# The last tile's 32-row stores on ScalarE's queue beside SyncE's

## The chip, the cores and the metric

The kernel runs on one core of a Trainium2 chip. The metric is the device time of one execution in microseconds (us).

## The reference

A block-sorted attention is followed by an affine mixer. What matters here is its last line, which gives the kernel's output of 4 batches × 768 tokens × 512 channels:

```python
def _moe_ref(x, alpha1, beta1, w_tok, alpha2, beta2, w_ch1, w_ch2, lam):
    ...
    ch = np.maximum(a2 @ w_ch1, 0.0) @ w_ch2
    return (u + lam * ch).astype(np.float32)
```

## The kernel before

The 768 tokens of a batch stand in six tiles of 128 rows. A tile holds 96 rows from the first 576 tokens and 32 rows from the last 192 (the "tail"), so a finished tile goes to the output in two stores, one of 96 rows and one of 32. The very last tile of the program is also cut by columns, into 384 and 128, so that the first part can be finished and stored while TensorE still multiplies the second. All output stores are issued by SyncE.

```python
    def moe_ch(b, hf, kks=range(3)):
        ...
            last = b == B - 1 and kt == NT - 1
            ost = att.tile([128, C], FT, name="ost", tag="ost", bufs=2)
            for lo, hi in ((0, 384), (384, C)) if last else ((0, C),):
                cps = psb([128, hi - lo], FT, "ch_ps")
                for m in range(HT):
                    pe.matmul(cps[:], hT[m][...], W2p[:, m, lo:hi], ...)   # cut
                dve.tensor_tensor(cps[:], cps[:], lamB[:, lo:hi], ALU.mult)
                dve.tensor_tensor(ost[:, lo:hi], cps[:], u_of[b][kt][:, lo:hi], ALU.add)
                nc.sync.dma_start(out[b, kt * 96:(kt + 1) * 96, lo:hi], ost[0:96, lo:hi])
                nc.sync.dma_start(out[b, TAIL + kt * 32:TAIL + (kt + 1) * 32, lo:hi], ost[96:128, lo:hi])
```

The softmax here doesn't subtract the row's maximum and nothing guards it: scores larger than these inputs give would overflow.

Of the kernel before, what the change touches and what calls it, by code (L numbers as in the profile page):

```python
# [16 lines left out]
def kernel(  # L17
# [20 lines left out]
    nc = tc.nc  # L38
# [13 lines left out]
    TAIL = 6 * BLK  # L52
# [35 lines left out]
    def psb(shape, dtype, name):  # L88
        return psB.tile(shape, dtype, name=name, tag="psB")

    def const(shape, dtype, name):
# [5 lines left out]
        out=ident16[:], in_=ident16[:], compare_op=ALU.not_equal, fill=1.0, base=0,  # L97
# [554 lines left out]
    def moe_ch(b, hf, kks=range(3)):  # L652
        hT = hT_of[(b, hf)]
        for kk in kks:
            kt = 3 * hf + kk
# [5 lines that stand above are left out]
                    pe.matmul(  # L661
                        cps[:], hT[m][:, kk * 128:(kk + 1) * 128], W2p[:, m, lo:hi],
                        start=(m == 0), stop=(m == HT - 1),
                    )
                dve.tensor_tensor(cps[:], cps[:], lamB[:, lo:hi], ALU.mult)
                dve.tensor_tensor(ost[:, lo:hi], cps[:], u_of[b][kt][:, lo:hi], ALU.add)
                nc.sync.dma_start(out[b, kt * 96:(kt + 1) * 96, lo:hi], ost[0:96, lo:hi])
                nc.sync.dma_start(out[b, TAIL + kt * 32:TAIL + (kt + 1) * 32, lo:hi], ost[96:128, lo:hi])


    ets = {}
# [86 lines left out]
    for kk in range(2):  # L758
        moe_ch(0, 0, (kk,))
        mix_k(1, gs=((0, 1), (2,))[kk])  # L760
        for h4 in range(2 * kk, 2 * kk + 2):
            turn_q(1, h4, dve.tensor_copy)
    pe.fixed = False
    for b in range(1, B):
        if b > 1:
            if b > 2:
                cross_q(b)
            mixing_matrices(b)
            mix_v(b)
            if b == 2:  # L770
                opened = pool.tensor_copy(gate[:], Vs[0][0:1, 0, 0:2])
                with tc.issue_after(opened.ins):
                    load_q(3)
                    load_raw(3, 1)
                    load_raw(3, 0)
            mix_k(b)
        emit_attention(b)
        if b == 1:
            moe_ch(0, 0, (2,))
        else:  # L780
            moe_h(b - 1, 0)
            moe_ch(b - 1, 0)
        moe_h(b - 1, 1)
        moe_a(b)
        moe_ch(b - 1, 1)
        if b == 1:
            load_q(2)
            cross_q(2)
# [33 lines left out]
```

## Time and profile before

| | before |
|---|---|
| median of 3 runs | 269.02 us (268.73 to 269.4) |
| span of the profiled execution | 266.8 us, granted clock 1.000 |
| TensorE (PE) busy | 257.3 us, 96% of the span |
| last matmul's end to the program's end | 4.30 us |

From the page of the kernel before, the line of PE's busy time (us, share of the span, instructions) and the line of the chain that ended last (share of the span by engine):

```profile
PE 257.3 (96%) x2049; PEld 141.6 (53%) x2059; DVE 154.8 (58%) x333; ACT 125.8 (47%) x232; POOL 92.6 (35%) x100
...
PE 89%; ACT 4%; DVE 4%; issue 1%; DMA 1%; DVEq 0%; ACTq 0%
```

TensorE bounds the kernel; no change to the last stores touches that. What they can change is the stretch after the last matmul. The timeline of that stretch in the kernel before follows (start in us from the span's start, duration in us, engine, line, operation, what it writes and reads; SPq is SyncE issuing a store, and ACTq, further on, ScalarE issuing one):

```profile
262.10 0.39 PE L65 MATMUL ch_ps<-W2p,hTb 128*128 128x128 bf16 x4
262.30 0.56 DVE L65 TENSOR_TENSOR ost<-ch_ps,u 128x384 f32<-128x384 f32 x1
...
262.89 0.32 SPq L667 DMA_DIRECT2D out_dram<-ost  x1
263.10 0.29 DVE L65 TENSOR_TENSOR ost<-ch_ps,u 128x128 f32<-128x128 f32 x1
263.26 0.42 SPq L668 DMA_DIRECT2D out_dram<-ost  x1
263.77 0.38 SPq L667 DMA_DIRECT2D out_dram<-ost  x1
264.20 0.43 SPq L668 DMA_DIRECT2D out_dram<-ost  x1
```

VectorE finishes the 384 columns at 262.86 and the 128 columns at 263.39 (263.10 + 0.29). The four stores leave one after the other. The last one is issued at 264.20, 0.8 us after its data were ready. More readings belong to it: the view of DMA issues (KB each, median us from issue to landing), SyncE's own waits (us in total, times, the longest), and the view by windows (the last two columns are the busy share of the 16 DMA engines and GB/s).

```profile
out_dram<-ost SPq DMA_DIRECT2D x1, 144.0 KB, 1.9
out_dram<-ost SPq DMA_DIRECT2D x2, 48.0 KB, 1.7
out_dram<-ost SPq DMA_DIRECT2D x1, 16.0 KB, 1.5
```

```profile
SPq L817 <- DMA out_dram<-ost: 0.6, 2, 0.3
```

```profile
264.25:264.50 0.25, 0.00 (x0) 0.00 (x0) 0.00 (x0) 0.00 (x0) 0.00 (x0) 1.00 0.62 203
264.50:264.75 0.25, 0.00 (x0) 0.00 (x0) 0.00 (x0) 0.00 (x0) 0.00 (x0) 1.00 0.27 74
264.75:265.00 0.25, 0.00 (x0) 0.00 (x0) 0.00 (x0) 0.00 (x0) 0.00 (x0) 1.00 0.52 135
265.00:265.25 0.25, 0.00 (x0) 0.00 (x0) 0.00 (x0) 0.00 (x0) 0.00 (x0) 1.00 0.21 49
```

(The two stores of 48 KB are one line here; 1.7 is the median of 1.74 and 1.61.) The last store, 16 KB, lands 1.5 us after its issue, at 265.7. SyncE hardly waits for landings (0.6 us): its last issue ends 1.24 us after VectorE's last result, until 1.49 us it checks other semaphores, and the first store has landed at 1.39 us. The DMA engines have a dip at 264.50 to 264.75: the first two stores are nearly done, and the third store's packets begin only at 264.64.

In this trace each of these stores raises its own semaphore by sixteen increments; its landing is the time of the sixteenth.

### The profile page before, as it was taken

The numbers are of one execution on the slowest core, as the hardware profiler recorded it, in microseconds if no ns is written. First come the engines' busy times: TensorE is split into PE (matmuls) and PEld (weight loads), VectorE is DVE, ScalarE is ACT, GpSimd is POOL, SyncE is SP. The second block draws the span as 40 slices with busy tenths as digits, with TensorE's granted clock in tenths as the row PEclk, the third lists the DMA queues.
The fourth block names the chain that finished last, engine by engine and source line by source line (L and its number), as shares of the span: only waits on it lengthen the run. The fifth ranks groups of instructions, "written<-read, shape, count | busy, mean of one in ns | idle before, by whom it ended". The sixth has DMA issues, their size and how long they took to land.

```text
span 266.8 us, 5147 instructions
## 1 busy us (share of the span) xinstructions
PE 257.3 (96%) x2049; PEld 141.6 (53%) x2059; DVE 154.8 (58%) x333; ACT 125.8 (47%) x232; POOL 92.6 (35%) x100
## 2 busy tenths in 40 slices
PE   7799999999999999999999999999999999999993
PEld 3467745565565444554565444554565445545542
DVE  6878687639567966722585867704675962042033
ACT  3376767642585312980375404970474305505600
POOL 8524789103585615008918125002409000000000
PEclk9999999999999999999999999999999999999999
DMA  6999999989999544499996342492200422012012
GB/s 80 183 208 252 206 211 207 209 209 118 206 165 146 115 83 120 115 83 95 207 196 135 61 100 80 118 109 51 81 1 2 86 71 79 2 39 79 2 39 79
DMA packets 62423, 30.88 MB, mean 116 GB/s; under 512 B 48888, under 2 KB 58112, under 8 KB 62400
## 3 DMA queue, kind: packets, MB, share of 16 engines
q0 software_dynamic: 23024, 15.60, 39.1%
q1 hardware_dynamic: 39376, 14.96, 32.7%
q8 instruction: 16, 0.26, 0.4%
q14 instruction: 7, 0.06, 0.1%
HBM read 32.78 MB, written 8.65 MB: 155 GB/s over the span
## 4 chain that ended last, share of the span: by engine, by line
PE 89%; ACT 4%; DVE 4%; issue 1%; DMA 1%; DVEq 0%; ACTq 0%
PE ch_ps L65 31%; PE h_ps L65 30%; PE tok_ps L65 12%; PE x_ps L65 5%; PE sc_ps L65 4%; ACT kT L65 2%; PE v_ps L65 2%; PE k_ps L65 1%; PE q_ps L65 1%; ACT et L65 1%; DVE csum L65 1%; DVE P L65 1%; PE m_ps L65 1%; DVE rsum L65 1%; PE wtok_ps L65 1%
## 5 line engine op out<-in xcount | busy, mean ns | idle before, releaser
L65 PE MATMUL h_ps<-a2T,W1p 128*128 128x384 bf16 x512 | 93.4, 326 | 0.2
L65 ACT ACTIVATE hTa<-h_ps 128x384 bf16<-128x384 f32 x96 | 45.9, 492 | 67.7 <-PE h_ps L65 66.6
L65 PE MATMUL ch_ps<-W2p,hTa 128*128 128x512 bf16 (+2 forms) x290 | 65.9, 370 | 0.5
L65 PEld LDWEIGHTS <-W1p 128*128 128x128 bf16 x512 | 47.5, 98 | 30.3 <-issue 0.9
L65 DVE TENSOR_TENSOR ch_ps<-ch_ps,lamB 128x512 f32<-128x512 f32 (+2 forms) x25 | 16.9, 676 | 62.8 <-PE ch_ps L65 60.1
L65 POOL TENSOR_SCALAR u<-b1lB,rs 128x512 f32<-128x512 f32 x18 | 28.9, 1612 | 64.7 <-DVE ost L65 60.1
L65 PEld LDWEIGHTS <-hTa 128*128 128x128 bf16 x300 | 28.7, 98 | 32.4
L65 PE MATMUL tok_ps<-x,w_tokT 128*128 128x512 f16 x144 | 32.1, 379 | 0.0
L65 POOL TENSOR_TENSOR u<-x,u 128x512 f32<-128x512 f16 x22 | 25.4, 1190 | 18.2 <-DVE x L65 17.3
L65 ACT ACTIVATE et<-sc_ps 96x768 f16<-96x768 f32 x32 | 24.9, 807 | 11.7 <-PE sc_ps L65 11.7
L65 ACT CAST u<-u 128x512 f16<-128x512 f32 x24 | 14.8, 618 | 25.7 <-DVE u L65 25.7
L65 PE MATMUL ch_ps<-W2p,hTb 128*128 128x512 bf16 (+2 forms) x100 | 25.0, 371 | 0.0
L65 PEld LDWEIGHTS <-w_tokT 128*128 128x128 f16 x180 | 14.8, 97 | 16.1
L65 DVE TENSOR_TENSOR tok_ps<-tok_ps,a1lB 128x512 f32<-128x512 f32 x24 | 16.6, 693 | 7.7 <-PE tok_ps L65 7.6
L65 DVE CAST kT<-k_ps 64x512 f16<-64x512 f32 x24 | 16.5, 688 | 3.4 <-PE k_ps L65 3.0
L65 DVE TENSOR_TENSOR x<-x_ps,recip 96x512 f16<-96x512 f32 (+2 forms) x32 | 17.6, 554 | 0.9
L65 DVE TENSOR_TENSOR u<-tok_ps,u 128x512 f32<-128x512 f32 x24 | 16.4, 689 | 1.7
L65 ACT ACTIVATE hTb<-h_ps 128x384 bf16<-128x384 f32 x32 | 15.3, 497 | 3.8 <-PE h_ps L65 3.4
L65 DVE TENSOR_TENSOR ost<-ch_ps,u 128x512 f32<-128x512 f32 (+2 forms) x25 | 16.6, 665 | 0.6
L65 POOL DMA_DIRECT2D qn<-in_q_dram x18 | 15.4, 872 | 4.2 <-PE q_ps L65 3.4
L65 PEld LDWEIGHTS <-hTb 128*128 128x128 bf16 x100 | 9.6, 98 | 10.9
L65 PEld LDWEIGHTS <-et 96*128 96x128 f16 (+2 forms) x288 | 12.4, 99 | 4.6 <-issue 1.2
(95 smaller groups left out, 214.0 us busy)
## 6 DMA issues: line engine op xcount, KB each, us to landing
out_dram<-ost SPq DMA_DIRECT2D x23, 192.0 KB, 2.2
raw<-in_v_dram POOLq DMA_DIRECT2D x8, 384.0 KB, 8.2
raw<-in_k_dram POOLq DMA_DIRECT2D x8, 384.0 KB, 10.7
vscr<-vA SPq DMA_DIRECT2D x6, 384.0 KB, 4.4
Vs<-vscr SPq DMA_DIRECT2D x6, 384.0 KB, 7.5
W1p<-in_moe_w_ch_dram POOLq DMA_DIRECT2D x4, 512.0 KB, 10.5
W2p<-in_moe_w_ch_dram POOLq DMA_DIRECT2D x4, 512.0 KB, 18.6
qn<-in_q_dram POOLq DMA_DIRECT2D x12, 128.0 KB, 5.8
```

Of the source, the lines that this page charges most:

```text
L65: ins = getattr(self.eng, name)(*args, **kwargs)
```

## The change

With two engines issuing, the 32-row store need not wait for the issue of the 96-row store, nor the second pair for the first. ScalarE has nothing else to do by then.

```diff
                 nc.sync.dma_start(out[b, kt * 96:(kt + 1) * 96, lo:hi], ost[0:96, lo:hi])
-                nc.sync.dma_start(out[b, TAIL + kt * 32:TAIL + (kt + 1) * 32, lo:hi], ost[96:128, lo:hi])
+                (nc.scalar if last else nc.sync).dma_start(
+                    out[b, TAIL + kt * 32:TAIL + (kt + 1) * 32, lo:hi], ost[96:128, lo:hi]
+                )
```

## The prediction

> **What bounds the kernel now.** TensorE. The page gives PE 257.3 us busy of a span of 266.8 us (96%), at a granted clock of 1.00 in the view of cores, and the chain that ended last is 89% PE. The change touches only the end. The timeline of the last microseconds reads: the last matmul group starts at 262.10 and takes 0.39 us; VectorE multiplies and adds the 384 columns (0.57 + 0.56 us, done 262.86), then the 128 columns (0.29 + 0.29 us, done about 263.39). SyncE issues four stores one after the other: 262.89 (96 rows, 384 columns, 0.32 us), 263.26 (32 rows, 0.42 us), 263.77 (96 rows, 128 columns, 0.38 us), 264.20 (32 rows, 0.43 us). The third store's data are ready at about 263.39, but SyncE is still busy with the second until 263.68. So serial issue holds the third store back by about 0.35 us, and the fourth by about 0.8 us. The DMA view gives 1.9, 1.7, 1.6 and 1.5 us from issue to landing; the fourth store therefore lands last, at about 265.7. Drains and barrier semaphores then run from 266.0 to 266.8.
>
> **What the change does.** It moves two of the four issues to ScalarE's queue (its last activation starts at 252.13). All bytes and all compute stay.
>
> **Cost.** The Trainium skill, "DMA: Bandwidth & Descriptors", section "Issuing engines are not separate DMA queues", says that all issuers share the same 16 DMA engines and that issuing from several saves only the sequencer's time. This trace agrees: issues of 0.32 to 0.43 us delay the last store, while the view by windows has the engines idle from 262.5 to 263.5. With two issuers I expect: 262.89 on both queues, then about 263.42 on both, each 0.3 to 0.45 us. The last issue starts 264.20 - 263.42 = 0.78 us earlier. Not all comes back: the stores now overlap more on the 16 engines (which already moved 250 to 290 GB/s from 263.75 to 264.25), so I take landing of the last stores to lengthen by 0.1 to 0.3 us. Gain on the span: about 0.5 us, estimated from these durations; all of it is on the critical path, as nothing else runs then. That is 0.2% of 269.02 us, about the spread of the three runs (268.73 to 269.4).
>
> What could eat it: the skill's "Perfetto Trace Analysis", section "DMA Instruction — HWDGE (DVE, Sync)", says the descriptor generator is locked for exclusive use by one issuer. The trace of before has no two such issuers to show it. If the lock covers most of an issue, the four issues still follow each other, the last starts at about 264.0, and the gain shrinks to 0.1 to 0.2 us.
>
> **Prediction.** 268.5 us, 8 in 10 between 267.9 and 269.2. Faster by over 2%: 1%. Within 2%: 97%. Slower by over 2%: 2%.
>
> **What would show it.** Right: two stores on ScalarE's queue starting within 0.1 us of SyncE's; the last issue near 263.4 instead of 264.2; last landing near 265.2; span near 266.3; PE busy unchanged. Lock story: issues on the two queues lengthened to 0.6 to 0.8 us, or staggered. Contention story: early issues but landings well over 1.9 us.
>
> **What would make it wrong.** An extra queue that costs setup or extra waits at the program's end; a scheduler that orders other instructions differently because two issues changed engine; a slow first issue on ScalarE of a microsecond or more. Within 2% stands unless these cost over 5 us.

## More of the kernel before

For finer comparisons I read the trace's records directly: the instructions' starts, the packets' times, and the semaphore increments.

## The result, and the profile after

| | before | after |
|---|---|---|
| median of 6 runs | 269.15 us (268.73 to 269.4) | 268.78 us (268.55 to 268.91) |
| ratio | | 0.9986, 95% interval 0.9973 to 0.9999 |
| span of the profiled execution | 266.8 us | 266.8 us |

A ratio is the mean time of one kernel's fast runs over the mean of the other's fast runs of the same rounds, so it is not quite the ratio of the medians. The verdict is "the same" (within 2%), at 0.37 us less by the medians. Five more rounds later (run again, below) gave a ratio of 1.0002, 0.9962 to 1.0042: a gain of this size cannot be resolved by timing, so what follows rests on the end of the traces.

In the two traces the work of TensorE, VectorE and GpSimd stands in the same order; on ScalarE two stores are added after its last activation, and the same two are missing on SyncE. In the first profile after, VectorE's last result came at 263.56, 0.17 us later than before, although nothing up to there had changed. Over the profiles that moment lies between 263.39 and 264.34 (in drop_two alone, profiled in an execution of 271.96 us at a mean clock of 0.986, at 267.1). That is more than the change moves, so the spans say nothing, and I count from VectorE's last result instead.

The timeline after, first the merged lines of the first and second store of each engine (x2), then from 263.45 on, so that the second stores stand alone:

```profile
262.47 0.56 DVE L65 TENSOR_TENSOR ost<-ch_ps,u 128x384 f32<-128x384 f32 x1
...
263.06 0.85 SPq L667 DMA_DIRECT2D out_dram<-ost  x2
263.06 0.91 ACTq L668 DMA_DIRECT2D out_dram<-ost  x2
```

```profile
263.27 0.29 DVE L65 TENSOR_TENSOR ost<-ch_ps,u 128x128 f32<-128x128 f32 x1
263.59 0.32 SPq L667 DMA_DIRECT2D out_dram<-ost  x1
263.59 0.38 ACTq L668 DMA_DIRECT2D out_dram<-ost  x1
```

Both engines issue at 263.06, and both issue again at 263.59, 0.03 us after VectorE's last result. The issues are as early as they can be. The last one comes 0.77 us sooner than before, counted from VectorE's last result. The same three views as before:

```profile
out_dram<-ost SPq DMA_DIRECT2D x1, 144.0 KB, 2.1
out_dram<-ost ACTq DMA_DIRECT2D x1, 48.0 KB, 2.2
out_dram<-ost SPq DMA_DIRECT2D x1, 48.0 KB, 1.9
out_dram<-ost ACTq DMA_DIRECT2D x1, 16.0 KB, 2.1
```

```profile
SPq L819 <- DMA out_dram<-ost: 1.5, 2, 1.2
```

```profile
264.25:264.50 0.25, 0.00 (x0) 0.00 (x0) 0.00 (x0) 0.00 (x0) 0.00 (x0) 1.00 0.98 289
264.50:264.75 0.25, 0.00 (x0) 0.00 (x0) 0.00 (x0) 0.00 (x0) 0.00 (x0) 1.00 0.91 281
264.75:265.00 0.25, 0.00 (x0) 0.00 (x0) 0.00 (x0) 0.00 (x0) 0.00 (x0) 1.00 0.48 129
265.00:265.25 0.25, 0.00 (x0) 0.00 (x0) 0.00 (x0) 0.00 (x0) 0.00 (x0) 1.00 0.02 6
```

The reader should see three things. The landings of all stores are longer (2.1, 2.2, 1.9 and 2.1 us instead of 1.9, 1.7, 1.6 and 1.5). SyncE's wait for landings grew from 0.6 to 1.5 us: the issue time that was saved became waiting. And the dip of the DMA engines at 264.50 to 264.75 is filled (share 0.91 instead of 0.27; 0.65 where the window is moved by the 0.17 us by which VectorE's last result is later): the stores now overlap on the engines.

The account in us after VectorE's last result, from the trace's records:

| | before | after | after, run again |
|---|---|---|---|
| last issue (16 KB) | 0.802 | 0.032 | 0.031 |
| its time to landing | 1.493 | 2.068 | 1.993 |
| last landing | 2.295 | 2.100 | 2.024 |
| last landing to the program's end | 1.103 | 1.157 | 1.152 |
| program's end | 3.398 | 3.257 | 3.176 |

Of 0.77 us, the longer landing takes back 0.58 or 0.50. Another 0.05 us goes after the landing: SyncE checks the semaphores one by one, about 0.06 us each, in an order fixed by the program. Before, three checks are left when the last landing is seen; after, four, because the store that lands last is checked one place earlier. What is left is 0.14 us in one profile and 0.22 us in the other (0.21 us in run primed, whose last tile is the same). The kernel before was profiled once.

### The profile page after: what moved, and what is told of

Same layout as the page of the kernel before. It is cut to its first block, busy times and chain, and to the rows that moved or that the text cites. A ratio compares the mean times of both kernels' runs of the same rounds, so it can differ in the third digit from the quotient of the medians.

```text
span 266.8 us, 5149 instructions
## 1 busy us (share of the span) xinstructions
PE 257.6 (97%) x2049; PEld 141.6 (53%) x2059; DVE 154.8 (58%) x333; ACT 125.8 (47%) x232; POOL 92.5 (35%) x100
## 4 chain that ended last, share of the span: by engine, by line
PE 89%; ACT 4%; DVE 4%; issue 1%; DMA 1%; DVEq 0%; ACTq 0%
PE ch_ps L65 31%; PE h_ps L65 30%; PE tok_ps L65 12%; PE x_ps L65 5%; PE sc_ps L65 4%; ACT kT L65 2%; PE v_ps L65 2%; PE k_ps L65 1%; PE q_ps L65 1%; ACT et L65 1%; DVE csum L65 1%; DVE P L65 1%; PE m_ps L65 1%; DVE rsum L65 1%; DMA P<-in_sort_net_dram 1%
```

## The experiments

The question is why the landing grew. Three theories: shared transfer (the stores' bytes queue behind one another on the 16 engines), a slow queue (ScalarE's queue, or its first store, is slower in itself), and the descriptor generator (the prediction's fear: only one engine at a time can have a transfer set up). Diffs are against the changed kernel. "End" is the time from VectorE's last result to the program's end, from one profile each. The kernel before was timed in the same rounds; all outputs were correct except where said. The runs come from three chips, which matters little for the tail: primed and again, with the same last tile on two of them, agree to 0.01 us.

| run | last issue | last landing | end | ratio to before (95%) |
|---|---|---|---|---|
| before | 0.80 | 2.30 | 3.40 | |
| after | 0.03 | 2.10 | 3.26 | 0.9986 (0.9973 to 0.9999) |
| again | 0.03 | 2.02 | 3.18 | 1.0002 (0.9962 to 1.0042) |
| drop_one | 0.40 | 1.89 | 3.11 | 0.9987 (0.9952 to 1.0022) |
| drop_two | 0.03 | 1.79 | 3.06 | 1.0004 (0.9958 to 1.0049) |
| swap | 0.03 | 1.91 | 3.07 | 0.9985 (0.9951 to 1.0020) |
| pieces_one | 2.64 | 4.12 | 5.46 | 1.0075 (1.0063 to 1.0087) |
| pieces_two | 0.87 | 2.53 | 3.66 | 1.0016 (1.0003 to 1.0028) |
| last_only | 0.37 | 2.00 | 3.10 | 0.9992 (0.9979 to 1.0005) |
| primed | 0.03 | 2.03 | 3.18 | 0.9994 (0.9980 to 1.0008) |
| act_only | 0.89 | 2.40 | 3.50 | 1.0002 (0.9973 to 1.0030) |

The three runs with cut VectorE work follow at the end; they are counted from the last matmul.

### again: the changed kernel once more

No edit.

> The changed kernel once more, for the size of its gain and for how far one profile differs from another. In the first profiles the last landing came 2.30 us after VectorE's last result before the change and 2.10 us after it, although the last issue came 0.77 us sooner. Expected if the profiles are typical: the same 2.1 us within 0.15 us, a last store that needs 2.0 to 2.1 us from issue to landing, and a time 0.1 to 0.4 us under the kernel before. If the first profile was an outlier, the landing takes 1.6 to 1.8 us.

The profile repeated: 2.02 us to the last landing, the 16 KB store at 1.99 us. The time did not show a gain (median 268.96 us against 268.86 us). The first profile was typical to 0.08 us. The two timings agree within their intervals, and together they show no gain that is clear of noise.

### pieces_one and pieces_two: is issuing parallel at all?

```diff
+                for n in range(4 if last else 0):
+                    row = kt * 96 + n * 32 if n < 3 else TAIL + kt * 32
+                    nc.sync.dma_start(                                  # pieces_one
+                    (nc.scalar if n % 2 else nc.sync).dma_start(        # pieces_two
+                        out[b, row:row + 32, lo:hi], ost[n * 32:(n + 1) * 32, lo:hi]
+                    )
                 # cut: the last tile skips the usual two stores
```

> The cost of issuing made large: the last tile's stores are cut into pieces of 32 rows, four for each part of the columns, eight in all, all on SyncE. Same bytes. All theories: eight issues of about 0.42 us one after another, the last about 2.6 us after VectorE's last result; last landing about 4.1 us after it; slower than the kernel before by about 1.7 us.

> The same eight pieces, every second one on ScalarE. If the two engines issue side by side, the last issue comes about 0.9 us after VectorE's last result and the time is 1.2 to 1.8 us under pieces_one. If the descriptor generator is held by one issuer for most of an issue, issues on both engines lengthen to about 0.8 us, or alternate, and the gain is under 0.4 us.

Medians: 270.92 us for one queue (1.95 us over the kernel before, where 1.7 was expected) and 269.51 us for two, a gain of 1.41 us as expected. The last issue of pieces_two lies at 0.87 us, also as expected. The timelines, first of pieces_one, then of pieces_two:

```profile
263.37 3.56 SPq L669 DMA_DIRECT2D out_dram<-ost  x8
```

```profile
263.26 1.71 SPq L669 DMA_DIRECT2D out_dram<-ost  x4
263.27 1.80 ACTq L669 DMA_DIRECT2D out_dram<-ost  x4
```

Eight issues in 3.56 us on one engine; four and four in 1.71 and 1.80 us on two. By the records, the issues of pieces_two took 0.31 to 0.43 us each on both engines, those of pieces_one 0.32 to 0.42. Nothing was locked out for an issue's length. So the change does what it intends, and with enough issues in a row it pays in time. But one thing shows already in the landings of pieces_two, although the pieces are all alike:

```profile
out_dram<-ost SPq DMA_DIRECT2D x2, 16.0 KB, 1.5
out_dram<-ost ACTq DMA_DIRECT2D x2, 16.0 KB, 1.7
```

A 16 KB piece on ScalarE needs 1.7 us, one on SyncE 1.5.

### drop_one and drop_two: without the bytes of the first part

```diff
+                if last and lo == 0:
+                    continue
```

That edit is in both, ahead of the stores; drop_one also issues the 32-row store from SyncE. The output is wrong: the last tile's first 384 columns are never written (the comparison gives not-a-number).

> Wrong on purpose: the last tile's two stores of the first 384 columns are left out; the two stores of the last 128 columns stay, both on SyncE. Control for drop_two. All theories: issues at about 0.03 and 0.4 us after VectorE's last result, landings 1.5 to 1.6 us after issue, so the last landing about 1.9 us after VectorE's last result.

> Wrong on purpose as drop_one, but the 32-row store of the last 128 columns is on ScalarE, its first and only store. Theory of shared transfer (the landing of the changed kernel is longer because the engines still move the 192 KB of the first 384 columns): with those bytes gone ScalarE's store lands 1.5 to 1.7 us after issue as SyncE's does, the last landing comes about 1.6 us after VectorE's last result, and the time is 0.25 to 0.4 us under drop_one. Theory of a slow queue (ScalarE's first store, or its queue, is slower in itself): it still lands 2.0 to 2.2 us after issue and drop_two is no faster than drop_one.

DMA issues of drop_one, then of drop_two:

```profile
out_dram<-ost SPq DMA_DIRECT2D x1, 48.0 KB, 1.5
out_dram<-ost SPq DMA_DIRECT2D x1, 16.0 KB, 1.5
```

```profile
out_dram<-ost SPq DMA_DIRECT2D x1, 48.0 KB, 1.6
out_dram<-ost ACTq DMA_DIRECT2D x1, 16.0 KB, 1.8
```

Neither theory got its whole number. With the 192 KB gone, ScalarE's 16 KB store lands after 1.756 us instead of 2.068 or 1.993, so those bytes account for 0.24 to 0.31 us. But it does not fall to the 1.494 us that the same store takes on SyncE in drop_one. Another 0.26 us is left, either of ScalarE's queue or of two stores going out side by side. (The profile of drop_two is of its slowest execution, but its tail looks like the others': VectorE's last result comes 0.907 us after the last matmul, 0.904 before, and the issues take 0.32 and 0.39 us.) The expected 0.25 to 0.4 us between the two kernels were missed: the ends differ by 0.05 us, and the times do not tell them apart.

### act_only: is ScalarE's queue slower in itself?

```diff
-                nc.sync.dma_start(out[b, kt * 96:(kt + 1) * 96, lo:hi], ost[0:96, lo:hi])
+                (nc.scalar if last else nc.sync).dma_start(out[b, kt * 96:(kt + 1) * 96, lo:hi], ost[0:96, lo:hi])
```

> All four stores of the last tile on ScalarE, issued one after the other as SyncE did before the change. So far ScalarE's packets began 0.97 to 0.98 us after issue, SyncE's 0.81 to 0.82 us, whenever the engines were free. If ScalarE's queue is slower in itself, its first store begins at 0.97 us here too and the last store (16 KB) lands 1.7 to 1.8 us after issue, so the last landing is about 2.5 us after VectorE's last result, 0.2 us later than in the kernel before. If the delay came only from two issuers asking for the descriptor generator at once, it begins at 0.82 us and lands 1.5 us after issue, as in the kernel before.

```profile
out_dram<-ost ACTq DMA_DIRECT2D x1, 144.0 KB, 1.9
out_dram<-ost ACTq DMA_DIRECT2D x2, 48.0 KB, 1.7
out_dram<-ost ACTq DMA_DIRECT2D x1, 16.0 KB, 1.5
```

Those are the landings of the kernel before, 1.9, 1.7 and 1.5 us, now on ScalarE. The last 16 KB store took 1.512 us (1.493 on SyncE), and the end came 0.11 us later than before, mostly because the issues themselves are a little longer (0.39 to 0.45 us) and the last starts 0.09 us later. The first store's packets began 0.89 us after issue, between the two numbers expected (0.82 on SyncE alone, 0.97 to 0.98 on ScalarE beside SyncE). So ScalarE's queue as such costs 0.02 us of landing for the last store and 0.05 us for the first. The slow-queue theory falls.

That leaves the two stores side by side as the cause of the 0.26 us. In drop_two the packets of the two stores do share the engines: SyncE's 96 packets of 512 B (six for each of 16 engines) took 0.033 us each, 0.2 us per engine, and ScalarE's last packet began 0.05 us after SyncE's last one. But ScalarE's packets also began 0.98 us after issue instead of 0.89. That 0.09 us could be the descriptor generator serving SyncE first, or packets queued on the engines; these runs do not tell.

The packets make up only part of the 0.26 us, though. A landing can be cut in two at the end of the store's last packet. In drop_two that end came 1.237 us after ScalarE's issue, against 1.139 us in drop_one: 0.10 us. The other 0.16 us passed after it, 0.519 us from the last packet's end to the landing instead of 0.355. Wherever one engine issued everything (before, drop_one, act_only, pieces_one, thirds_one), each store of the last tile needed 0.34 to 0.39 us for this last stretch (packets given to stores in order of time); ScalarE's last 32-row store beside SyncE's stores needed 0.50 to 0.60 us. What lengthens this stretch stays open; the packets do not show it.

### primed: is it the first store on ScalarE?

```diff
-                (nc.scalar if last else nc.sync).dma_start(
+                (nc.scalar if b == B - 1 and kt > 2 else nc.sync).dma_start(
```

> As the changed kernel, and also the 32-row stores of the two tiles before the last are on ScalarE, so that the last tile's are not its first. If a first store on ScalarE is slow, the early ones take it and the last tile's 32-row store of 384 columns begins its packets about 0.8 us after issue instead of 1.3 us, and the last landing comes 0.2 to 0.5 us sooner. Shared transfer: the last tile as in the changed kernel.

The last tile was the same as in run again to 0.01 us: end 3.18, 16 KB store 2.00 us. ScalarE's 32-row store of 384 columns again began its packets 1.34 us after issue. A first use costs nothing here.

### swap: which store on which engine

```diff
-                nc.sync.dma_start(out[b, kt * 96:(kt + 1) * 96, lo:hi], ost[0:96, lo:hi])
-                (nc.scalar if last else nc.sync).dma_start(
-                    out[b, TAIL + kt * 32:TAIL + (kt + 1) * 32, lo:hi], ost[96:128, lo:hi]
-                )
+                (nc.scalar if last else nc.sync).dma_start(out[b, kt * 96:(kt + 1) * 96, lo:hi], ost[0:96, lo:hi])
+                nc.sync.dma_start(out[b, TAIL + kt * 32:TAIL + (kt + 1) * 32, lo:hi], ost[96:128, lo:hi])
```

> The 96-row stores on ScalarE and the 32-row stores on SyncE. Shared transfer: the last landing as in the changed kernel, 2.1 us after VectorE's last result within 0.1 us, the time equal within noise. Slow queue: the large stores start their packets 0.4 to 0.5 us later than on SyncE (1.3 us after issue instead of 0.8 us), and everything lands that much later, so slower than the changed kernel by 0.3 to 0.5 us. Descriptor generator kept by one issuer: whichever issue starts second has its packets late, on either engine.

```profile
out_dram<-ost ACTq DMA_DIRECT2D x1, 144.0 KB, 2.0
out_dram<-ost SPq DMA_DIRECT2D x1, 48.0 KB, 1.7
out_dram<-ost ACTq DMA_DIRECT2D x1, 48.0 KB, 1.9
out_dram<-ost SPq DMA_DIRECT2D x1, 16.0 KB, 1.7
```

ScalarE's 144 KB store began its packets 0.97 us after issue, not 1.3. So the 1.34 us of the changed kernel (0.83 us after VectorE's last result) was no property of ScalarE: there its 48 KB stood behind SyncE's 144 KB, whose 96 packets began 0.52 us sooner and kept each engine busy for six packets of 0.094 us, 0.56 us. In swap the small store goes first and hardly holds up the large one. The last landing was 1.91 us, 0.1 to 0.2 us better than in the changed kernel, where I had expected the same within 0.1 us; with one profile I do not build on it. The 16 KB store, now on SyncE, landed 1.705 us after issue, against 1.99 to 2.07 us on ScalarE in the changed kernel, beside the same other stores. So side by side the two engines are not alike, although each alone is; the runs do not show whether it is the engine or the order of the stores.

### last_only: half of the change

```diff
-                (nc.scalar if last else nc.sync).dma_start(
+                (nc.scalar if last and lo else nc.sync).dma_start(
```

> Half of the change: only the 32-row store of the last 128 columns goes to ScalarE; SyncE keeps the other three. The 96-row store of the last columns is again issued 0.37 us after VectorE's last result. Shared transfer: landing about 1.7 to 1.9 us after that issue, last landing 2.1 to 2.2 us after VectorE's last result, between the two kernels or equal to the changed one. Slow first store on ScalarE: its store lands 2.0 us or more after issue and still is done in time, so the same; then the profile tells them apart by the start of its packets, 1.1 to 1.3 us after issue instead of 0.8 to 0.9.

```profile
out_dram<-ost SPq DMA_DIRECT2D x1, 144.0 KB, 1.9
out_dram<-ost SPq DMA_DIRECT2D x2, 48.0 KB, 1.7
out_dram<-ost ACTq DMA_DIRECT2D x1, 16.0 KB, 1.8
```

The last landing came at 2.00 us, somewhat sooner than expected, although the last issue is 0.34 us later than in the changed kernel. It is SyncE's 96-row store, 1.62 us after its issue: a later issue, and a shorter landing. This is the exchange in one pair of numbers. ScalarE's 16 KB store, with the 192 KB of the first part ahead but SyncE's 48 KB behind it, needed 1.795 us, 0.28 us more than in act_only: 0.09 us before its last packet's end and 0.20 us after it, much as in drop_two. In this one profile half of the change has all of its gain: end 3.10 us, against 3.18 and 3.26 for the whole.

### thirds_one, thirds_two, thirds_swap: send the first bytes sooner

```diff
-                dve.tensor_tensor(cps[:], cps[:], lamB[:, lo:hi], ALU.mult)
-                dve.tensor_tensor(ost[:, lo:hi], cps[:], u_of[b][kt][:, lo:hi], ALU.add)
+                cuts = ((0, 192), (192, 384)) if last and lo == 0 else ((lo, hi),)
+                for c, d in cuts:
+                    dve.tensor_tensor(cps[:, c - lo:d - lo], cps[:, c - lo:d - lo], lamB[:, c:d], ALU.mult)
+                for c, d in cuts:
+                    dve.tensor_tensor(ost[:, c:d], cps[:, c - lo:d - lo], u_of[b][kt][:, c:d], ALU.add)
+                    ...  # both stores of columns c:d; queues as the name says
```

> VectorE's two operations on the first 384 columns cut into halves of 192, each half stored as soon as it is done; six stores, all on SyncE. More issues on one engine: the first store goes out about 0.5 us sooner, but six issues of about 0.4 us end about 0.8 us after VectorE's last result as before, or later. End of the last matmul to the end of the program: as the kernel before (4.30 us) within 0.15 us.

> The same six stores, 32-row stores on ScalarE. If the bytes of the first 384 columns are what the last stores wait behind, then with half of them sent about 0.5 us sooner the last store lands 1.75 to 1.85 us after issue instead of 2.0 to 2.1 us; the end comes 3.8 to 4.0 us after the last matmul (4.30 us before the change, 4.08 to 4.16 us after it), a candidate to beat both kernels by 0.1 to 0.4 us, which the times may not resolve.

> As thirds_two with the 96-row stores on ScalarE and the 32-row stores on SyncE, since in the swap run the last landing came at 1.91 us instead of 2.02 to 2.10 us after VectorE's last result. Expected: the end 0.05 to 0.15 us sooner than thirds_two; if the difference of swap was chance, the same within 0.08 us, which is how far the two profiles of the changed kernel lie apart.

These were misses. From the last matmul's end to the program's end: before 4.30 us, after 4.16 and 4.08, thirds_one 5.08, thirds_two 4.19, thirds_swap 4.14. No half went out sooner, and in thirds_one the sixth issue started 1.47 us after VectorE's last result, not 0.8. The timeline of thirds_two:

```profile
261.77 0.77 DVE L65 TENSOR_TENSOR ch_ps<-ch_ps,lamB 128x192 f32<-128x192 f32 x2 [1.17 <-PE ch_ps L65]
...
262.58 0.62 DVE L65 TENSOR_TENSOR ost<-ch_ps,u 128x192 f32<-128x192 f32 x2
262.96 1.27 SPq L670 DMA_DIRECT2D out_dram<-ost  x3
262.97 1.33 ACTq L671 DMA_DIRECT2D out_dram<-ost  x3
```

Two multiplies of 192 columns take 0.77 us together, where one of 384 takes 0.57, and the first half is stored 1.19 us after VectorE's first multiply began (262.96 - 261.77), just as the undivided part was (262.89 - 261.70). VectorE's last result came 1.17 us after the last matmul instead of 0.90. The landing did shorten as the transfer theory wants, to 1.79 us for the 16 KB store, but the cut had lengthened the chain ahead of it. thirds_swap was 0.05 us better than thirds_two, within the spread of repeated profiles. Medians: 269.63, 269.14 and 268.64 us, against 268.73 us for the kernel before. None is clear of noise against the kernel before. Of the runs in the table with correct output, swap and last_only have the shortest ends (3.07 and 3.10 us), by less than the timing can resolve.

## Why the prediction was right or wrong

The time was right: 268.5 us was predicted, 268.78 us measured, within the range and within 2%. That says little for the reasoning: the range (267.9 to 269.2) also held the time with no gain at all, 269.15 us. The steps fared as follows.

- **TensorE bounds the kernel, and only the end is touched.** Right: PE 257.6 us after, 257.3 before.
- **Two issuers start together, the last issue 0.78 us sooner.** Right: 0.77 us, both engines within 0.004 us of each other. This is what the Trainium skill says in "DMA: Bandwidth & Descriptors", section "Issuing engines are not separate DMA queues": several issuers save only issue time. pieces_one and pieces_two agree, with 1.41 us saved, and so does act_only: all issues on ScalarE alone are no faster.
- **"I take landing of the last stores to lengthen by 0.1 to 0.3 us."** This is the term that was mis-sized. It was 0.58 us in one profile and 0.50 us in the other. The parts, for the 16 KB store:

| 16 KB store | issue to landing, us | of it, to the end of its last packet | from there to landing |
|---|---|---|---|
| SyncE, issues one after the other (before; drop_one) | 1.493; 1.494 | 1.153; 1.139 | 0.340; 0.355 |
| ScalarE, issues one after the other (act_only) | 1.512 | 1.173 | 0.339 |
| ScalarE, beside SyncE's 48 KB only (drop_two) | 1.756 | 1.237 | 0.519 |
| ScalarE, 192 KB ahead, SyncE's 48 KB behind (last_only) | 1.795 | 1.261 | 0.534 |
| ScalarE, beside 48 KB and with 192 KB ahead (after; again; primed) | 2.068; 1.993; 2.002 | 1.466; 1.447; 1.447 | 0.602; 0.546; 0.555 |
| SyncE, beside ScalarE's 48 KB and with 192 KB ahead (swap) | 1.705 | 1.296 | 0.409 |

  In the order of the runs the queue costs 0.02, the neighbour 0.24, the bytes ahead 0.24 to 0.31 (by last_only, 0.28). I had thought of the bytes ahead and not of the neighbour. By the other cut, 0.29 to 0.31 of the 0.50 to 0.58 us lie before the last packet's end and 0.21 to 0.26 after it. That the growth comes from stores sharing the engines is thus shown for most of the first part (0.09 us of it is the later start that stays open); for the second it is shown only that it appears when two engines issue side by side. The swap row says that the sum holds for this assignment of stores to engines, not for any.
- **Last landing near 265.2, span near 266.3.** Wrong: 265.66 and 266.8. Of that, 0.17 us is the later VectorE result of that execution; the rest is the landing.
- **The generator's lock might eat the gain.** Not in the form feared. "Perfetto Trace Analysis", section "DMA Instruction — HWDGE (DVE, Sync)", says that it is locked for exclusive use, and that the recorded issue includes the wait for it. Issues on two engines at once took 0.31 to 0.43 us, as alone. Whether it causes the 0.09 us by which ScalarE's packets start later beside SyncE stays open.
- **Gain about 0.5 us.** The first timing gave 0.37 us, the second none, the two traces 0.14 and 0.22 us. The traces' numbers are those I trust more, though the kernel before has only one profile; by them the gain is under half of what was predicted, while the predicted time stands because both are small against the range.

## What to carry to other kernels

Issuing the last stores from a second engine takes the issue time off the end only until the stores meet on the DMA engines: count the bytes still ahead of the last store, and the store that goes out beside it, before you count the issue time that you save. When the end is one short burst, look at where the DMA engines dip between stores; that dip (a busy share of 0.27 at 264.50 to 264.75 here) is the room that earlier issues can fill. Where many small stores are issued in a row, the second queue can be worth most of half the issue time (here 1.41 us of eight issues' 3.56 us).

## What the Trainium skill lacked or had wrong

- "DMA: Bandwidth & Descriptors", section "Issuing engines are not separate DMA queues": it says that issue time is saved, not that landings grow in return. Here a 16 KB store grew from 1.49 to 2.0 or 2.1 us, and 0.20 to 0.27 us of 0.77 us saved were left at the last landing.
- The same page, "Latency and other measured facts", gives HWDGE a first-byte latency of about 0.6 us. Here the first packets began 0.81 to 0.82 us after an issue's recorded start on SyncE, 0.89 us on ScalarE alone and 0.97 to 0.98 us on ScalarE beside SyncE. The page doesn't say from where its number is counted.
- "Perfetto Trace Analysis", section "DMA Instruction — HWDGE (DVE, Sync)": it has the lock held until all descriptors are made, but gives no duration for it. Two engines issuing at once showed no longer issues (0.31 to 0.43 us against 0.32 to 0.42 us), so a wait for the lock does not show in these records.
- In the pages I read I found nothing on this: on SyncE an issue right behind another took longer than one after a pause, whatever its rows. In pieces_one the first 32-row store took 0.315 us and the next three 0.41 to 0.42 us; in swap, where SyncE paused between them, both of its 32-row stores took 0.314 us.
- Also not found there: at the program's end SyncE checks the semaphores one after another, about 0.06 us each, so the order in which the last landings are checked moves the end by that much per place (three checks left before the change, four after it).
